# Moving one load to GpSimd's DMA queue and rebuilding the last transpose of the first chunk's output

## The chip, the cores and the metric

The kernel runs on one core of a Trainium2 chip. The metric is device microseconds of one execution, taken as the median of several. The engines of the core are named as in the profile: PE is TensorE (PEld its weight loads), DVE is VectorE, ACT is ScalarE, POOL is GpSimd, SP is SyncE. A "q" behind an engine's name (SPq, POOLq) is its sequencer, which issues DMAs.

## The reference, cut to what matters

An mLSTM cell over 4 batches, 8 heads, 768 time steps and head size 40, whose output feeds a two-layer network with a sigmoid-approximated GELU:

```
for t in range(S):                                    # S = 768, per batch and head
    m_new  = max(f[t] + m, i[t])
    f_stab = exp(f[t] + m - m_new); i_stab = exp(i[t] - m_new); m = m_new
    C = f_stab * C + i_stab * outer(v[t], k[t])       # 40 x 40
    n = f_stab * n + i_stab * k[t]
    y[t] = sigmoid(o[t]) * (C @ q[t]) / max(|n . q[t]|, 1)
x = y.transpose(0, 2, 1, 3).reshape(3072, 320)        # 8 heads x 40 = 320 features
h = x @ w_in                                          # 320 -> 2048
out = (h * sigmoid(1.702 * h)) @ w_out                # 2048 -> 320
```

All of it is in float32.

## The kernel before, in words

Time is cut into six chunks `w` of 128 steps. A chunk holds 4 batches of 128 steps, so 512 tokens, and 32 pairs of batch and head. Attention of a chunk is computed in matrix form (scores, weights, values and a carried state), and its output `y` (steps x 320 features, per batch) is turned into `xT` (features x tokens) for the network. While PE does the network of chunk `w`, the other engines prepare the attention of chunk `w + 1`. The order on every engine is written out by hand (`manual_schedule`): instructions stand on an engine in the order in which the program emits them.

**The first chunk's turn.** For `w = 0`, `outputs` writes `y` (L478), and `seam` transposes it on PE with the identity (L531): features 0, 2, 4, ... of the first 256, then 1, 3, 5, ..., then the last 64 features. The third transpose has 128 columns, because `outputs` also writes a copy of features 256 to 319 behind them (L482, on POOL, for the last batch on DVE). So the last 64 features come out twice, on partitions 0 to 63 and 64 to 127, as a later product wants them. All three transposes write one PSUM tile `p_x` of the pool `ps_a` (two buffers). ACT copies them to `xT` (L537). For the last batch DVE copies the first 128 columns (L534) and ACT the other 256 (L535). Then `up(0, 0)` starts the network: `full` (L620) runs over the halves `n` of the tokens, and half 1 of the very first weight block needs the last batch. Each such f32 product is two MATMUL rows in the profile. `rest` (L629) uses the last 64 features.

**The weights.** `w_in` and `w_out` come from DRAM with a wider layout and are rebuilt in 20 pieces by `convert`: two ACT operations (L243, L247) and four DVE operations (L256, L257, L259, L265) for a piece. Pieces 0 to 9 are `w_in`, 10 to 19 `w_out`. `fetch` issues their DMAs on SP.

**The loads.** SP issues nearly all of them, in the order of the program. Behind the first chunk's attention SP issues `load_gates(1)` (L92), `load(1, "k")` (L120), `load_squares(1, "q")` (L108), the first three `w_out` pieces (L167), and at `j == 1` of the network's loop `load(1, "v")` (L120), then further pieces, and at `j == 4` `spread(1)` (L403). Each DMA of an engine's queues takes the next of eight completion counts, and first waits until the DMA that held this count before it has landed; SP and ACT share one set of eight, POOL's queue has its own eight.

**POOL in this stretch.** At `j == 1` POOL runs `wait_for` (L586, it waits for a piece of `w_in`) and `scale(0, 1)` (L582, it reads `v_st`). At `j == 3` POOL's queue issues the DMAs of `gates(1)` (L304, L307, L330, L331) and of `columns_in(1)` (L350, L352), which lead to `columns_turn(1)` on DVE (L356).

**The queries of the second chunk.** `load_squares(1, "q")` fills the tile `q_sq` with four DMAs of 32 partitions x 16 x 160 numbers, 320 KB each. They are used by `block_transposes` on DVE (L394) at `j` 4 and 5, and twice more behind the loop.

Of the kernel before, what the change touches and what calls it, by code (L numbers as in the profile page):

```python
# [8 lines left out]
FP = mybir.dt.float32  # L9
# [8 lines left out]
L = 128  # L18
# [8 lines left out]
def kernel(  # L27
# [12 lines left out]
    nc = tc.nc  # L40
    B, H, S, D = q.shape
    BH = B * H
    DM = H * D
# [23 lines left out]
    ps_m = ctx.enter_context(tc.tile_pool(name="ps_m", bufs=4, space=PSUM))  # L67
    ctx.enter_context(tc.manual_schedule())

    V, A, G, T = nc.vector, nc.scalar, nc.gpsimd, nc.tensor  # L70
# [24 lines left out]
    def k_of(w):  # L95
        return (k_0, k_1)[w] if w < 2 else k_st[:, 0:BH * D].rearrange("s (h d) -> s h d", d=D)
# [2 lines left out]

        return k_of(w)[t, h, :] if w < 2 else k_st[t, h * D:h * D + DP]  # L100

    def load_squares(w, what):
        for dst, src in [((k_sq, k), (q_sq, q))["kq".index(c)] for c in what]:
            x = src[:, :, w * L:(w + 1) * L, :].rearrange("b (p two) (r c) d -> two r (b p) (c d)", two=2, c=4)
            for i in range(2):
                for n in range(2):
                    r, at = slice(i * 64 + n * 32, i * 64 + n * 32 + 32), (1 - n) * 32
                    nc.sync.dma_start(out=dst[r, at:at + BH // 2 * 4 * D].rearrange("r (j x) -> r j x", x=4 * D), in_=x[i])  # L108

    def load(w, what, bs=slice(0, B)):  # L110
        hs = slice(bs.start * H, bs.stop * H)
        for c in what:
            if c == "o" and w not in eo:
                eo[w] = ld.tile([L, BH, D], FP, tag="eo", bufs=1, name="eo")
            dst, src = {"k": (k_of(w), k), "q": (q_st, q), "v": (v_st, v), "o": (eo.get(w), o_gate)}[c]
            if w and c in "kv":
                for i, t, r in ((0, slice(0, L), slice(0, L)), (1, slice(0, HL), slice(HL, L)),
                                (1, slice(HL, L), slice(0, HL))):
                    x = src[:, :, w * L + t.start:w * L + t.stop, :].rearrange("b (p two) s d -> two s (b p) d", two=2)
                    nc.sync.dma_start(out=dst[r, i::2, 0:D], in_=x[i])  # L120
                continue
            nc.sync.dma_start(out=dst[:, hs, 0:D],
                              in_=src[bs, :, w * L:(w + 1) * L, :].rearrange("b h s d -> s (b h) d"))
# [74 lines left out]
    ident = const.tile([128, 128], FP, name="ident")  # L198
# [28 lines left out]
    kT, qT, ys, xT, gs, o_ps, sums, vw, x_row = {}, {}, {}, {}, {}, {}, {}, {}, {}  # L227
# [109 lines left out]
    def banks(name):  # L337
        return ps_a.tile([128, 2, 512], FP, tag="a", name=name)
# [125 lines left out]
    def outputs(w, hs, u):  # L464

        n = hs.stop - hs.start
        c, b = divmod(hs.start // H, 2)
        den = work.tile([L, n, 1], FP, tag="den", name="den")
        V.tensor_scalar(out=den, in0=u[:, :, D:D1], scalar1=-1.0, scalar2=1.0, op0=OP.mult, op1=OP.max)
        V.tensor_tensor(out=den, in0=u[:, :, D:D1], in1=den, op=OP.max)  # L470
        V.reciprocal(out=den, in_=den)
        z = eo[w][:, hs, :]
        V.scalar_tensor_tensor(out=z, in0=z, scalar=1.0, in1=u[:, :, 0:D], op0=OP.add, op1=OP.mult)
        if b == 0:
            ys[w, c] = work.tile([L, 2, DM + 64], FP, tag="y", name="y")
        for x in range(n // H):
            y, h = ys[w, c][:, b + x], slice(hs.start + x * H, hs.start + x * H + H)
            V.scalar_tensor_tensor(out=y[:, 0:DM].rearrange("p (h d) -> p h d", d=D), in0=eo[w][:, h, :], scalar=0.5,  # L478
                                   in1=den[:, x * H:(x + 1) * H].to_broadcast([L, H, D]), op0=OP.mult, op1=OP.mult)
        if w == 0:  # L480
            y = ys[w, c][:, b:b + n // H]
            (V if hs.stop == BH else G).tensor_copy(out=y[:, :, DM:DM + 64], in_=y[:, :, DM - 64:DM])  # L482

    def values(w, c):
        if w == 0:
# [35 lines left out]
    def x_of(w):  # L521
        if w not in xT:
            xT[w] = work.tile([128, 3, B, L], FP, tag="xT", bufs=1, name="xT")
        return xT[w]

    def seam(w, c, b):
        px = banks("p_x")[:, 0, 0:3 * L]
        y = ys[w, c][:, b, :]
        for x in range(3):
            y_x = y[:, 256:384] if x == 2 else y[:, x:256:2]  # L530
            T.transpose(px[:, x * L:(x + 1) * L], y_x, ident)  # L531
        to, px = x_of(w)[:, :, 2 * c + b, :], px.rearrange("r (x t) -> r x t", t=L)
        if 2 * c + b == B - 1:
            V.tensor_copy(out=to[:, 0], in_=px[:, 0])  # L534
            A.copy(out=to[:, 1:3], in_=px[:, 1:3])  # L535
        else:
            A.copy(out=to, in_=px)  # L537

    def x_square(c, n):

# [35 lines left out]
    def scale(w, c, part=0, parts=1):  # L576
        n = PH // parts
        hs = slice(c * PH + part * n, c * PH + (part + 1) * n)
        if part == 0:
            vw[w, c] = work.tile([L, PH, D1], FP, tag="u", name="vw")  # L580
        e = cols[w][:, 2 * BH + hs.start:2 * BH + hs.stop].unsqueeze(2).to_broadcast([L, n, D1])
        G.tensor_tensor(out=vw[w, c][:, part * n:(part + 1) * n], in0=v_st[:, hs, :], in1=e, op=OP.mult)  # L582
# [282 lines left out]
            convert_add(0)  # L865
    load_gates(1)
    load(1, "k")
    load_squares(1, "q")
    open_first(2)
    values(0, 2)  # L870
    open_first(3)
# [26 lines left out]
    for w in range(NW):  # L898
        more = w + 1 < NW
        if w == 0:  # L900
            for j in range(NF // 2):
                if j % 2 == 0:
                    ahead, behind = converted[j // 2]
                    run([(convert, p) for p in ahead] + [(fetch, p) for p in fetched.get(j // 2, ())])
                    up(w, j, lambda: run([(columns_turn, 1) if p is None else (convert, p) for p in behind]))
                if j == 6:
                    load(1, "o")
                if j == 1:
                    wait_for(w_in_sb[:, 1, 512:1024])
                    scale(0, 1)  # L910
                    load(1, "v")
                if j < B and j % 2:
                    carry(0, j // 2)
                if j == 3:
                    masks()
                    gates(1)
                    columns_in(1)
                if j == 4:
                    spread(1)
                if j >= B:  # L920
                    transposes(1, j - B)
                if j in (4, 5):
                    block_transposes(1, 2 * j - 7)
        else:
            token_sums(w)
            if more:
                gates(w + 1)
                load(w + 1, "o")
            for j in range(NF // 2):
                up_fast(w, j)  # L930
                if w == 1 and j < 4:
                    weight_sums(j)
                if more and j == 2:
                    load(w + 1, "vk")
                    columns_in(w + 1)
                    spread(w + 1)
                if more and j:
                    for n in ((), (0, 2), (4,), (6, 1), (3,), (5, 7), ())[j - 1]:
                        block_transposes(w + 1, n)
                if more and j == 7:  # L940
                    columns_turn(w + 1)
                if 2 <= j < 6:
                    hidden_difference(w, j - 2)
                if j >= 6:
                    hidden_sums(w, (j - 6,), G)
            gelu_fast(w, NF // 2 - 1)
            hidden_sums(w, (2, 3), V)
        side = attention(w + 1) if more else {}
        if w == 0:
            block_transposes(1, 5)  # L950
            block_transposes(1, 7)

            blocks = [(lambda b=b, n=n: down(w, b, n)) for n0 in (0, 2) for b in range(B) for n in (n0, n0 + 1)]
        else:
            blocks = down_fast(w, 0) + down_fast(w, 1)
        for i, block in enumerate(blocks):
            if w == 0 and i in (0, 4, 5):
                convert((17, 18, 19)[max(i - 3, 0)])
            if w + 2 < NW and i == (6 if w == 0 else 0):
                load_gates(w + 2)  # L960
            if w + 2 < NW and i == 13:
                load_squares(w + 2, "kq" if w else "k")
            if w == 0 and i == 15:
                load_squares(w + 2, "q")
            block()
            run(side.get(i, []))
            if w == 0 and i in (11, 13):
                input_sums(slice(0, 4) if i == 11 else slice(4, 8))
# [30 lines left out]
```

## Time and profile before

| what | us |
|---|---|
| median of three runs (468.34 to 468.99) | 468.94 |
| the profiled execution | 467.52 |
| its span, first to last instruction | 465.8 |
| PE busy in the span | 459.9 |
| DVE busy | 340.9 |
| ACT busy | 189.3 |
| POOL busy | 163.9 |
| mean granted TensorE clock | 1.000 |

The profile is one execution of the program; its own time is 1.72 us more than its span. Durations and instants below are of that execution, in us from the span's start. The span also comes in 40 slices of 11.6 us, in which a digit is the busy share of an engine in tenths. A row of the timeline gives the start, the length, the engine and line, the operation with its shape, how many instructions were merged, and in brackets how long the engine was idle before and what released it. The chain of waits is followed back from the last instruction, at each step to what released it.

### The profile page before, as it was taken

The page shows a single profiled execution, that of the slowest core. Times are in us where ns is not written, and L with a number is a line of the kernel's source. Part 1 is how long each engine was busy: PE and PEld are TensorE (multiplying, and loading weights), DVE is VectorE, ACT ScalarE, POOL GpSimd, SP SyncE. Part 2 cuts the span into 40 slices and gives each one's busy share as a digit, 9 for nine tenths or more (in the row PEclk, how much of TensorE's full clock was granted, in tenths as well). Part 3 has the DMA queues.
Part 4 walks back from the last instruction along what each step waited for, and adds up shares of the span by engine and source line. Part 5 has one row for each costly group of instructions (what it writes and reads, how often), then busy time and mean ns, then how long its engine had stood idle before and what let it go on. Part 6 is the DMA issues. An engine that isn't in the chain of part 4 may idle for free.

```text
span 465.8 us, 12359 instructions
## 1 busy us (share of the span) xinstructions
PE 459.9 (99%) x5063; PEld 387.9 (83%) x5063; DVE 340.9 (73%) x699; ACT 189.3 (41%) x431; POOL 163.9 (35%) x153
## 2 busy tenths in 40 slices
PE   8999999999999999999999999999999999999996
PEld 6867887776769999678999678999878999877996
DVE  5788999799779777688875688876768867535622
ACT  4676769200546500554700554900444810354100
POOL 5101417100898600365700266700248510157100
PEclk9999999999999999999999999999999999999999
DMA  8999998049993036997024998024999305000000
GB/s 166 210 308 159 206 301 180 3 94 185 156 154 97 14 76 141 188 134 139 3 65 127 194 136 161 6 56 103 198 136 107 90 18 139 28 1 0 1 29 30
DMA packets 135561, 52.87 MB, mean 113 GB/s; under 512 B 101984, under 2 KB 131632, under 8 KB 135504
## 3 DMA queue, kind: packets, MB, share of 16 engines
q1 hardware_dynamic: 127136, 50.27, 54.9%
q10 hardware_dynamic: 8048, 1.66, 1.8%
q8 instruction: 40, 0.66, 0.7%
q0 software_dynamic: 320, 0.15, 0.2%
q14 instruction: 17, 0.14, 0.1%
HBM read 44.52 MB, written 7.54 MB: 112 GB/s over the span
## 4 chain that ended last, share of the span: by engine, by line
PE 94%; SPq 1%; DVE 1%; POOL 1%; DMA 1%; ACT 0%; issue 0%; DVEq 0%
PE p_out L812 33%; PE p_h L703 25%; PE p_h L711 8%; PE p_out L758 8%; PE p_h L620 6%; PE p_c L596 3%; PE p_o L503 2%; PE p_s L459 2%; PE p_i L511 2%; PE p_h L629 2%; PE p_t L386 1%; PE p_s L448 1%; SPq L120 1%; DMA k_sq<-in_k_dram 1%; PE p_o L493 0%; PE p_w L415 0%
## 5 line engine op out<-in xcount | busy, mean ns | idle before, releaser
L749 POOL TENSOR_TENSOR g<-g,parts 128x512 f32<-128x512 f32 x30 | 38.3, 1278 | 190.2 <-DVE parts L741 182.8
L737 ACT COPY parts<-p_h 128x256 f32<-128x256 f32 x40 | 14.9, 373 | 150.3 <-PE p_h L703 147.0
L812 PE MATMUL p_out<-w_out_sb,g 128*128 128x160 f32 x480 | 69.6, 301 | 0.1
L812 PEld LDWEIGHTS p_out<-w_out_sb,g 128*128 128x128 f32 x480 | 66.5, 190 | 1.2 <-ACT g L684 0.4
L703 PE MATMUL p_h<-xT,w_in_sb 128*128 128x256 f32 x240 | 67.0, 388 | 0.0
L684 ACT ACTIVATE g<-g 128x512 f32<-128x512 f32 x80 | 50.1, 631 | 40.0 <-DVE g L744 24.2
L703 PEld LDWEIGHTS p_h<-xT,w_in_sb 128*128 128x128 f32 x240 | 43.8, 190 | 18.5 <-issue 7.5
L817 DVE TENSOR_TENSOR o_sb<-o_sb,p_out 128x160 f32<-128x160 f32 x70 | 21.4, 317 | 41.1 <-PE p_out L812 40.5
L812 PE MATMUL p_out<-t_sb,s 128*128 128x160 f32 x320 | 47.2, 300 | 0.0
L740 DVE TENSOR_TENSOR t_x<-p_h,parts 128x256 f32<-128x256 f32 x40 | 16.7, 418 | 39.3 <-PE p_h L711 33.2
L812 PEld LDWEIGHTS p_out<-t_sb,s 128*128 128x128 f32 x320 | 44.4, 190 | 0.2
L703 PE MATMUL p_h<-t_x,s_in 128*128 128x256 f32 x160 | 41.1, 379 | 0.0
L711 PE MATMUL p_h<-xT,w_in_x 64*128 64x512 f32 (+1 forms) x192 | 39.8, 540 | 0.0
L435 ACT ACTIVATE wt<-wt,cols 128x64 f32<-128x64 f32 x160 | 38.8, 333 | 0.1
L758 PE MATMUL p_out<-w_out_sb,g 128*128 128x320 f32 x128 | 35.7, 436 | 0.0
L703 PEld LDWEIGHTS p_h<-t_x,s_in 128*128 128x128 f32 x160 | 30.4, 190 | 4.2
L758 PEld LDWEIGHTS p_out<-w_out_sb,g 128*128 128x128 f32 x128 | 23.9, 190 | 9.5
L741 DVE TENSOR_TENSOR parts<-p_h,t_x 128x512 f32<-128x512 f32 x40 | 27.7, 692 | 3.6
L748 ACT COPY g<-p_h 128x512 f32<-128x512 f32 x30 | 17.4, 580 | 30.7 <-PE p_h L711 25.3
L620 PE MATMUL p_h<-xT,w_in_sb 128*128 128x256 f32 x128 | 29.8, 385 | 0.0
L711 PEld LDWEIGHTS p_h<-xT,w_in_x 64*128 64x128 f32 x192 | 16.9, 186 | 14.7 <-issue 13.7
L744 DVE TENSOR_TENSOR g<-p_h,parts 128x512 f32<-128x512 f32 x40 | 27.7, 691 | 1.4
(197 smaller groups left out, 841.1 us busy)
## 6 DMA issues: line engine op xcount, KB each, us to landing
q_sq<-in_q_dram SPq DMA_DIRECT2D x20, 320.0 KB, 10.2
wt<-m_row SPq DMA_DIRECT2D x20, 256.0 KB, 5.5
k_sq<-in_k_dram SPq DMA_DIRECT2D x16, 320.0 KB, 6.0
out_dram<-o_sb SPq DMA_DIRECT2D x24, 160.0 KB, 1.9
eo<-in_o_gate_dram SPq DMA_DIRECT2D x5, 640.0 KB, 8.1
bits<-in_moe_w_in_dram SPq DMA_DIRECT2D x6, 512.0 KB, 10.5
q_sq<-x_row SPq DMA_DIRECT2D x10, 256.0 KB, 2.8
v_st<-in_v_dram SPq DMA_DIRECT2D x14, 160.0 KB, 5.1
```

Of the source, the lines that this page charges most:

```text
L435: A.activation(out=x[:, h, :], in_=x[:, h, :], func=AF.Exp, scale=-1.0, bias=cols[w][:, c * PH + h:c * PH + h + 1])
L620: T.matmul(ph[j][i][:, t], w_in_sb[:, c, f * 128:(f + 1) * 128], x[:, c, t], start=(first and c == 0 and n == 0), stop=(not first and c == ...
L684: A.activation(out=gs[w, j][:, i, :], in_=gs[w, j][:, i, :], func=AF.Gelu_apprx_sigmoid)
L703: T.matmul(out, a, x[n], start=start, stop=stop)
L711: T.matmul(row[:, t], w_in_x[r, j, :], rest_x[r, 2, t], start=(not late and h == 0), stop=(late and h == n - 1))
L741: V.tensor_tensor(out=y[:, half_w:3 * half_w].rearrange("p (a t) -> p a t", a=2), in0=flat[:, half_w:3 * half_w].rearrange("p (a t) -> p a ...
L744: V.tensor_tensor(out=g[:, 1, :], in0=row1, in1=y[:, half_w:3 * half_w], op=OP.add)
L748: A.copy(out=g[:, 0, :], in_=row0)
L749: G.tensor_tensor(out=g0, in0=g0, in1=u, op=OP.add)
L758: T.matmul(po, gs[w, f // 2][:, f % 2, b * L:(b + 1) * L], w_out_sb[:, f, :], start=(f == 0), stop=(f == NF - 1))
L812: T.matmul(po, a(f), b[:, f, :], start=(f == 0), stop=(f == NH - 1))
L817: V.tensor_tensor(out=dst, in0=x, in1=po, op=OP.add)
```

## The change

Three edits. The load of the second chunk's queries leaves SP's queue and is issued by POOL's queue, behind `scale(0, 1)` at `j == 1`. DVE's copy of the last 64 features in `outputs` goes for the last batch of the first chunk. And `seam` has a path of its own for that batch: the first transpose writes a PSUM tile of the pool `ps_m` (four buffers), the second writes `p_x`, the third takes only 64 columns; ACT then copies the second with one operation, and the third with two, once to partitions 0 to 63 and once to 64 to 127.

```diff
-    def load_squares(w, what):
+    def load_squares(w, what, queue=nc.sync):
...
-                    nc.sync.dma_start(out=dst[r, at:at + BH // 2 * 4 * D].rearrange("r (j x) -> r j x", x=4 * D), in_=x[i])
+                    queue.dma_start(out=dst[r, at:at + BH // 2 * 4 * D].rearrange("r (j x) -> r j x", x=4 * D), in_=x[i])
...
-        if w == 0:
+        if w == 0 and hs.stop < BH:
             y = ys[w, c][:, b:b + n // H]
-            (V if hs.stop == BH else G).tensor_copy(out=y[:, :, DM:DM + 64], in_=y[:, :, DM - 64:DM])
+            G.tensor_copy(out=y[:, :, DM:DM + 64], in_=y[:, :, DM - 64:DM])
...
     def seam(w, c, b):
+        y, to = ys[w, c][:, b, :], x_of(w)[:, :, 2 * c + b, :]
+        if 2 * c + b == B - 1:
+            first = ps_m.tile([128, L], FP, tag="m", name="p_x")
+            T.transpose(first, y[:, 0:256:2], ident)
+            px = banks("p_x")[:, 0, 0:2 * L]
+            T.transpose(px[:, 0:L], y[:, 1:256:2], ident)
+            T.transpose(px[0:64, L:2 * L], y[:, 256:DM], ident)
+            V.tensor_copy(out=to[:, 0], in_=first)
+            A.copy(out=to[:, 1], in_=px[:, 0:L])
+            for r in (0, 64):
+                A.copy(out=to[r:r + 64, 2], in_=px[0:64, L:2 * L])
+            return
         px = banks("p_x")[:, 0, 0:3 * L]
-        y = ys[w, c][:, b, :]
         for x in range(3):
             y_x = y[:, 256:384] if x == 2 else y[:, x:256:2]
             T.transpose(px[:, x * L:(x + 1) * L], y_x, ident)
-        to, px = x_of(w)[:, :, 2 * c + b, :], px.rearrange("r (x t) -> r x t", t=L)
-        if 2 * c + b == B - 1:
-            V.tensor_copy(out=to[:, 0], in_=px[:, 0])
-            A.copy(out=to[:, 1:3], in_=px[:, 1:3])
-        else:
-            A.copy(out=to, in_=px)
+        A.copy(out=to, in_=px.rearrange("r (x t) -> r x t", t=L))
...
     load_gates(1)
     load(1, "k")
-    load_squares(1, "q")
     open_first(2)
...
                     wait_for(w_in_sb[:, 1, 512:1024])
                     scale(0, 1)
+                    load_squares(1, "q", G)
                     load(1, "v")
```

## The prediction, made before the changed kernel was run

> **What bounds the kernel now.** I read the page first: shares of the span, then slices.
>
> ```profile
> PE 459.9 (99%) x5063; PEld 387.9 (83%) x5063; DVE 340.9 (73%) x699; ACT 189.3 (41%) x431; POOL 163.9 (35%) x153
> PE   8999999999999999999999999999999999999996
> DMA  8999998049993036997024998024999305000000
> ```
>
> PE works through every slice but the first and last; the DMA engines are full in the first six. So time can be won where PE stands still, or lost by making PE wait. The second view, the busy time by stages, says where PE stands still (busy us and instruction counts of PE, PEld, DVE, ACT, POOL; then clock, DMA share, GB/s):
>
> ```profile
> 0.00:27.16 27.16, 24.92 (x314) 19.33 (x314) 17.95 (x53) 15.11 (x31) 8.80 (x27) 1.00 0.95 215
> 27.16:110.50 83.34, 83.34 (x895) 63.40 (x896) 73.81 (x140) 45.33 (x98) 18.12 (x20) 1.00 0.74 168
> ```
>
> From 27.16 to 110.50 PE has no gap. Both moved loads and all their users lie in there. Ahead of 27.16 PE lacks 2.24 us, most of it at the start. What is left is the turn. Third view, the chain of waits around it, in order of time:
>
> ```profile
> 25.46 0.50 DVE y L478
> 25.96 0.14 issue
> 26.10 0.59 PE p_x L531 x3
> 26.68 0.43 PE p_h L620 x2
> 27.12 0.04 issue
> 27.16 4.99 PE p_h L620 x22
> ```
>
> And the timeline of the same instants:
>
> ```profile
> 25.98 0.19 DVE L482 COPY y<-y 128x64 f32<-128x64 f32 x1
> 26.72 0.29 DVE L534 COPY xT<-p_x 128x128 f32<-128x128 f32 x1 [0.54 <-PE p_x L531]
> 27.05 0.37 ACT L535 COPY xT<-p_x 128x256 f32<-128x256 f32 x1 [0.62 <-DVE xT L534]
> 27.13 0.30 PEld L620 LDWEIGHTS p_h<-xT,w_in_sb 128*128 128x128 f32 x2 [0.41 <-issue]
> ```
>
> DVE's copy L534 starts when all three transposes are through (26.69), ACT's only when DVE has left the tile (27.01). PE has done half 0 of the first block (two rows from 26.52) and starts half 1 at 27.16, 0.15 behind L534's end. Rows of L620 follow each other every 0.227 (4.99 / 22), so without a wait half 1 would start at 26.52 + 0.454 = 26.97.
>
> **The change part by part.**
>
> *DVE's copy L482 (0.19).* It ended at 26.17; DVE then sat idle until 26.72 for the transposes. Worth nothing on the path: the transposes hide it. Without that cover it would be 0.19.
>
> *The third transpose.* 64 columns for 128. The three rows of L531 took 0.59 together, some 0.13 to 0.2 of pitch each; half a weight load less is between 0 and 0.1; I take 0.05. So half 0 starts at 26.47.
>
> *The separate tile.* The instruction order of the changed kernel shows DVE's copy waiting for the first transpose alone. That one starts at 26.10 and takes 0.27 to 0.39 by the rows of L531 (median 0.283), so the copy runs from 26.42 (0.03 for the release, as now) to 26.71, and half 1 may start at 26.71 + 0.15 = 26.86. PE itself is there at 26.47 + 0.454 = 26.92. PE no longer waits, and half 1 starts 0.24 earlier. Bounds: with nothing from the smaller transpose it is 26.97, 0.19 earlier; with 0.1 from it 26.87, 0.29 earlier. I take 0.24.
>
> *ACT's three copies for one.* 128x384 took 0.48 and 128x256 0.373, so 128 columns cost about 0.27, with a pitch of 0.17 to 0.27 (the two L537 in a row: 0.86 for 2 x 0.48). They start behind the third transpose, at about 26.67 rather than 27.05, and end at 27.28 to 27.5, against 27.42. The first user of the second 128 features is the 17th row of L620, at 26.47 + 16 x 0.227 = 30.1; of the last 64, L629 near 31.9. Cover 2.6 us or more. ACT's next, L247, feeds DVE's L265 (now 28.67): no later than now. If that cover went, it would cost at most 0.2.
>
> *What is late next.* DVE's conversions start 0.30 earlier (L256 follows L534), so `w_in_x` is ready at about 31.4, for 31.72 now, and L629 wants it at about 31.85. Pieces 3 and 4 (ready 36.42) stand before 36.98 and move likewise. The new tile shifts the round of four `ps_m` buffers by one: the fourth product tile now waits for DVE's copy (26.71) and is first written by row 13, near 29.2. Nothing in PE's next 83 us binds, so the 0.24 travels to the end.
>
> *SP without the four q issues (2.74 us, 38.37 to 41.11).* The `w_out` pieces, the v load, the next pieces and the spread move forward by up to that. ACT waited for such DMAs 1.19 us (until 50.15) and 3.82 us (until 61.98), and those waits shrink; but PE did not wait in that stretch, so this is worth 0. v's tile is free once POOL's L582 ends at 38.04. Late k would cost: PE transposes it from 56.2, it lands by about 44 now, and even all 1.28 MB of q ahead of it, at the stage's 168 GB/s, is 8 us.
>
> *POOL with the four issues.* They stand behind `scale(0, 1)`, so from about 38.05. Nothing on POOL is queued behind them until 50.12:
>
> ```profile
> 36.76 1.28 POOL L582 TENSOR_TENSOR vw<-v_st,cols 128x656 f32<-128x656 f32 x1
> 50.12 0.68 POOL L304 DMA_DIRECT2D m_row<-m_run  x1 [12.08 <-DVE m_run L296]
> 52.45 0.70 POOL L330 DMA_DIRECT2D st_row<-f_run  x1
> 56.38 2.42 POOL L350 DMA_DIRECT2D raw<-st_row  x4 [2.72 <-DMA st_row<-f_run]
> 57.10 0.43 DVE L257 TENSOR_SCALAR w_out_sb<-w_out_sb 128x512 uint32<-128x512 uint32 x1
> 61.35 2.06 DVE L394 STREAM_TRANSPOSE qT<-q_sq 128x512 f32<-128x512 f32 x2
> ```
>
> POOL's issues in this trace take 0.52 to 1.15 each, the nearest in pieces being L330 with 384 runs of 128 bytes (0.70); a q load has 512 runs of 640 bytes. Four are 2.1 to 4.6 us, I take 3: done at 41, 9 us before L304. Landing: L330 took 3.6 us, the q loads on SP 5.8 to 8.3 here and 10.2 in the median of all. I take 10: the last lands near 51. Bounds 42 and 55. Who needs them: DVE's L394 at 61.35, and, by the turns on eight counts, L331 at 53.15 waits for the first q load and the four L350 at 56.38 for the others. Both behind the expected landing. If L350 were late, L356 on DVE (70.31) would be next; its data now land at about 65.
>
> *DVE beside POOL's issues.* L257 at 36.80 took 1.53, not 0.43: it stood behind POOL's L582. POOL's DMA issues do not show that: L257 at 57.10, in the middle of L350, took 0.43, and the issues stayed at 0.55 to 0.80. The Trainium skill, "SBUF — State Buffer", section "Who interferes with whom", speaks against this edit: GpSimd writes the descriptors of its DMAs through a port that such VectorE operations lock, and the loser waits. By it q could lag by a few operations of 0.43, estimated at 4 x 0.43 = 1.7 us, still inside the cover, so its sum would be the same. From the rows alone: even four DVE operations held up for a whole 0.70 (2.8 us) meet 1.22 us of DVE idle at 42.2 and piece 9, ready 54.38 for 57.27 on PE.
>
> Sum: 0 + 0.24 + 0 + 0 = 0.24 us. The profiled execution would take 467.52 - 0.24 = 467.28. It lay 1.42 below the median of the runs shown, so on that scale 468.94 - 0.24 = 468.70.
>
> **The rivals.** A measurement of this kernel can tell about 0.2% from no change, 0.94 us.
>
> *Slower: POOL's queue delivers q late.* The place is DVE's L394. It stalls from 61.35, and behind it stand pieces 13 and 14 of `w_out`. Piece 14 is ready at 68.03 (its L265) and PE, whose first 32 rows of L758 take 8.62 from 67.34, wants it with the 13th, at 67.34 + 12 x 0.269 = 70.57. So it decides from a landing at 61.35 + 2.5 = 63.9, 26 us after the issue, and each us beyond is one of the kernel: at 30 us of transfer about 4 us, 473. For it: DMA digits of 9 in slices 1 to 5 (11.6 to 69.9), a queue that moved only 0.15 MB so far, and the same counts that chain L331 and L350 to q. Against: 3.6 to 6.2 us to landing on that queue in the same stretch, and 20 us of cover. 15%.
>
> *Faster beyond 0.94: SP's relief reaches PE.* Only if the 5.0 us of ACT waits fed a gap of PE; between 27.16 and 110.50 it has none, in the next stage 0.15 us. By the rows it is 0.24 + 0.15 at most, 468.55. What could carry it over is what the rows don't explain: the profiled execution lay 1.42 us below the median. A median moved by 0.7 to 1 gives about 467.8. 14%.
>
> *It does not do what it says: L534 still ends last.* If the copy is no earlier, half 1 stays at 27.16 or PE is set by another release: 468.9. 11%, inside 0.2%.
>
> **How the numbers follow.** The forecast (0.1 to 0.4 us won, 468.5 to 468.85, and the scatter of 0.65 between runs around it) has 60%. With the third rival, within 0.2% has 71%. Faster 14%, slower 15%. To hold 8 in 10 the range takes all within 0.2% and the near part of both other cases: 467.8 to 470.2, the upper end being q 1.5 us behind the deciding point.
>
> **What would show it.** Right: DVE's 128x128 copy starts near 26.4, ACT's first of three starts near 26.7, no longer behind DVE's, L620 rows follow every 0.227 from the first; POOLq has four q issues from 38 to 41; the `w_out` issues start near 38.4; POOL's `m_row` issue stays near 50; the stage from 27 to 110 shows no PE gap. Wrong: a stall of DVE ahead of the query transposes near 61, `raw` issues later than 57, or a PE gap between 56 and 90.

## The result, and the profile after

| | median, us | range | runs |
|---|---|---|---|
| before | 469.00 | 467.33 to 473.87 | 20 |
| after | 469.78 | 467.39 to 475.33 | 20 |

The ratio is 1.0015, with a 95% interval from 0.9994 to 1.0037: no difference that this measurement can tell. The profiled execution of the changed kernel took 469.14 us, its span 467.4.

The page, read as before: shares of the span, and the slices.

```profile
PE 460.4 (99%) x5063; PEld 387.4 (83%) x5063; DVE 341.7 (73%) x698; ACT 189.6 (41%) x433; POOL 165.2 (35%) x157
PE   8999999999999999999999999999999999999997
DMA  8999999028995034988124999114999405000000
```

At this scale PE looks the same; of the DMA digits, the seventh is 9 where it was 8, and some later ones move too. The busy time by stages shows more (columns as before):

```profile
0.00:27.16 27.16, 25.07 (x318) 19.52 (x319) 18.75 (x54) 16.26 (x34) 8.90 (x27) 1.00 0.93 192
27.16:110.50 83.34, 81.70 (x884) 61.23 (x883) 71.61 (x133) 44.29 (x97) 19.67 (x24) 1.00 0.79 171
```

PE had no gap in the second stretch; now it lacks 1.64 us (83.34 less 81.70). The timeline of the turn shows that the turn is not to blame:

```profile
24.69 0.49 DVE L478 SCALAR_TENSOR_TENSOR y<-eo,den 128x320 f32<-128x320 f32 x1
...
25.24 0.38 PE L530 MATMUL p_x<-ident,y 128*128 128x128 f32 x1 [0.47 <-DVE y L478]
...
25.66 0.29 DVE L534 COPY xT<-p_x 128x128 f32<-128x128 f32 x1 [0.48 <-PE p_x L530]
...
25.89 0.27 ACT L535 COPY xT<-p_x 128x128 f32<-128x128 f32 x1 [0.22 <-PE p_x L533]
26.05 0.53 ACT L537 COPY xT<-p_x 64x128 f32<-64x128 f32 x2
```

DVE's copy waits for the first transpose (L530) alone, and ACT's copies no longer for DVE. The chain of waits has the 24 rows of the first block in one piece, where before it had two rows, a stop and 22:

```profile
25.85 5.23 PE p_h L626 x24
```

From the end of `y` (25.19) to the end of the 24 rows (31.08) are 5.89 us. Before, they were 6.19 (25.96 to 32.15). The turn won 0.30.

So where does PE stand? The waits of PE from 56 to 90 (us in total, times, longest), and behind them the chain of the same stretch, cut to its DMA and the steps that follow it:

```profile
PE p_out L764 <- ACT g L641: 0.7, 1, 0.7
PE p_c L602 <- POOL vw L588: 0.5, 1, 0.5
PE p_out L764 <- DVE w_out_sb L265: 0.3, 1, 0.3
```

```profile
60.67 5.14 DMA bits<-in_moe_w_out_dram
...
74.06 0.58 ACT t_sb L247
...
75.95 0.27 ACT cols L367
...
77.61 1.29 POOL vw L588
...
78.94 1.14 PE p_c L602 x64
```

Read it from the bottom. PE's carry (L602) waits for POOL's `vw`, which waits for the columns that ACT makes (L367). ACT works in order, and the columns stand behind its conversions of the `w_out` pieces 13 to 17; the first of these waits for its DMA until 65.8 (before: until 61.98). The same lateness holds ACT's gelu (L641) back, which PE wants at 67. Before, the carry (there L596) followed the product without a gap, with `vw` ready in time. This is the chain before:

```profile
67.34 8.62 PE p_out L758 x32
75.96 2.01 PE p_c L596 x128
```

SP's issues after, and two of its rows before, show when the pieces go out:

```profile
40.60 11.81 SPq L167 DMA_DIRECT2D s_in<-in_moe_w_out_dram  x7
53.31 6.13 SPq L120 DMA_DIRECT2D v_st<-in_v_dram  x3
59.49 6.33 SPq L167 DMA_DIRECT2D bits<-in_moe_w_out_dram  x10
65.87 0.43 SPq L167 DMA_DIRECT2D t_sb<-in_moe_w_out_dram  x1
```

```profile
48.96 5.44 SPq L120 DMA_DIRECT2D v_st<-in_v_dram  x3
54.46 7.43 SPq L167 DMA_DIRECT2D bits<-in_moe_w_out_dram  x10
```

Relieved of the four query issues, SP should have been early. Instead the seven `w_out` issues took 11.81 us (before: 6.66), v followed at 53.31 (before: 48.96), the pieces 13 to 17 (`bits`, `t_sb`) at 59.49 and 65.87 (before: 54.46 and 61.93).

Busy time hides part of this: short waits lie inside the merged rows (the 16 rows of L635 took 2.54 us, where L629 before took 2.00; the carry 2.40 for 2.08). A cleaner yardstick, used below, is the **stretch**: from the start of the last `y` (L478) to PE's first product behind the carry (L758, in kernels with the new turn L764). Before, it ran from 25.46 to 77.89, so 52.43 us; after, from 24.69 to 80.01, so 55.32.

### The profile page after: what moved, and what is told of

Its sections match the earlier page's. It is cut to its first block, busy times and chain, and to the rows that moved or that the text cites. A ratio compares the mean times of both kernels' runs of the same rounds, so it can differ in the third digit from the quotient of the medians.

```text
span 467.4 us, 12367 instructions
## 1 busy us (share of the span) xinstructions
PE 460.4 (99%) x5063; PEld 387.4 (83%) x5063; DVE 341.7 (73%) x698; ACT 189.6 (41%) x433; POOL 165.2 (35%) x157
## 3 DMA queue, kind: packets, MB, share of 16 engines
q1 hardware_dynamic: 125024, 48.96, 54.3%
## 4 chain that ended last, share of the span: by engine, by line
PE 92%; ACT 2%; POOL 1%; DMA 1%; issue 1%; SPq 1%; DVE 1%; POOLq 0%; ACTq 0%; DVEq 0%
PE p_out L818 33%; PE p_h L709 27%; PE p_h L717 8%; PE p_out L764 6%; PE p_h L626 5%; PE p_c L602 2%; PE p_o L503 2%; PE p_s L459 2%; PE p_i L511 2%; PE p_h L635 1%; DMA bits<-in_moe_w_out_dram 1%; PE p_t L386 1%; PE p_s L448 1%; SPq L120 1%; ACT w_out_sb L243 0%
## 5 line engine op out<-in xcount | busy, mean ns | idle before, releaser
L764 PE MATMUL p_out<-w_out_sb,g 128*128 128x320 f32 x128 | 36.1, 437 | 1.0 <-ACT g L641 0.7
L764 PEld LDWEIGHTS p_out<-w_out_sb,g 128*128 128x128 f32 x128 | 23.9, 190 | 11.1 <-ACT g L641 0.9
L626 PE MATMUL p_h<-xT,w_in_sb 128*128 128x256 f32 x128 | 29.7, 385 | 0.0
```

Source lines behind the costliest of these rows:

```text
L626: T.matmul(ph[j][i][:, t], w_in_sb[:, c, f * 128:(f + 1) * 128], x[:, c, t], start=(first and c == 0 and n == 0), stop=(not first and c == ...
L764: T.matmul(po, gs[w, f // 2][:, f % 2, b * L:(b + 1) * L], w_out_sb[:, f, :], start=(f == 0), stop=(f == NF - 1))
```

## The experiments

**First round: each half, and both kernels again.** Theory A: the transfers of the first chunk are a second bound, and queries issued on POOL's queue, beside the others, make the pieces late. Theory B: both kernels scatter in this stretch, and the profile of before was a lucky one. Theory C: POOL's issues hold DVE up.

`before_again` and `after_again` have no edit. `seam_only` is the kernel before with the new turn and without the copy; `q_only` is the kernel before with this alone:

```diff
-    load_squares(1, "q")
...
                     scale(0, 1)
+                    load_squares(1, "q", G)
                     load(1, "v")
```

> The kernel before, unchanged, for the scatter between executions. Theory A (crowding): in the changed kernel POOL's query loads share the DMA engines with the second chunk's keys and the first w_out pieces that SP issues; the keys land late, SP's queue, which waits for the DMA eight back, falls behind, the w_out pieces come some 4 us late and PE stands still for 1 to 3 us between 60 and 80 us. By A this run looks like the first profile of before: the 160 KB key loads land within 4 to 9 us, the first v load is issued near 49, PE has no gap above 0.3 us from 30 to 110. Rival B (scatter): the late DMAs of the changed kernel's profile were one slow execution; by B this run may show them as well, a first v load at 51 or later and PE gaps of 1 us or more. Time ratio to before 1.000, interval within 0.003 of it.

> The changed kernel, unchanged, a second look. A: again the 160 KB key loads take 12 us or more to land, the first v load is issued at 52 or later, ACT's first w_out conversion waits for its DMA, PE stands still for 1 to 3 us in sum between 56 and 80. B: the DMAs may be on time, and then PE has no gap there and the span is 0.2 to 0.4 us under that of before. Time ratio 1.000 to 1.004 by A, 0.999 to 1.000 by B.

> The turn of the changed kernel, the query load back on SP at its old place. Both theories: no wait between the first two rows and the later rows of the first product after the turn, 0.2 to 0.3 us won against before from the end of y to row 3; PE without a gap above 0.3 us to 110; the first v load issued near 49. Time ratio 0.998 to 1.000.

> The query load on POOL's queue, the turn as before. A: keys and w_out pieces late as in the changed kernel, the first v load at 52 or later, PE gaps of 1 to 3 us between 56 and 80, ratio 1.002 to 1.006. B: nothing but scatter, ratio 1.000, no PE gap. A third theory C, that POOL's descriptor writing holds up DVE, would show DVE's two-port operations between 37 and 41 much longer than 0.43 and DVE, not a DMA, as the releaser of PE's waits.

| | median, us | ratio to before, 95% | start of `y` | stretch | mean clock |
|---|---|---|---|---|---|
| before_again | 468.73 | 0.9981 [0.9958, 1.0003] | 24.37 | 53.62 | 1.000 |
| after_again | 469.87 | 1.0001 [0.9975, 1.0028] | 25.25 | 55.60 | 0.993 |
| seam_only | 469.05 | 0.9985 [0.9963, 1.0008] | 25.06 | 53.87 | 1.000 |
| q_only | 469.67 | 1.0010 [0.9980, 1.0040] | 25.44 | 57.72 | 0.992 |

All ratios include 1, so the times alone tell nothing. As for the traces, B is half right: before_again, the same code, has a stretch 1.2 us longer than the first profile of before, and `y` itself starts anywhere from 24.4 to 25.5, which is more than the turn can win. A has the two longest stretches, both with the queries on POOL's queue. Their first `w_out` issues did come early, at 38.44 and 38.91 (before_again 41.65), but the loads took 9.8 to 13.6 us to land (before_again 5.9 to 9.4), and the second v issue stood until the last v issue at 54.34 and 55.67 (before_again 54.17): SP's lead was gone. Yet this doesn't show A. These two executions were the second slowest and the slowest of the 12 of their kernel (471.99 and 473.40 us), and before_again's was the second fastest (467.57). Signs that A had named failed too: the keys of after_again landed after 6.9 to 10.1 us, not 12 or more; the first v load went out at 44.31 and 46.16, not at 52 or later; and seam_only, for which both theories wanted a v load near 49 and no PE gap above 0.3 us, issued it at 51.58 and had a gap of 0.7. C has no row behind it: no wait of PE above 0.4 us ends on DVE.

**Second round: lighten the load, or move its victim.** `no_q` drops the added line from the changed kernel, so that the queries are not loaded at all. The three `early_cols` kernels (on the kernel before, on seam_only, on the kernel after) put DVE's transposition of the columns ahead of its work on pieces 14 to 16, and piece 17 behind the columns in ACT's order:

```diff
-    converted = {0: ((3, 4), (5,)), 1: ((6,), (7, 8)), 2: ((9, 10), (11, 12)), 3: ((13,), (14, 15, None, 16))}
+    converted = {0: ((3, 4), (5,)), 1: ((6,), (7, 8)), 2: ((9, 10), (11, 12)), 3: ((13,), (None, 14, 15, 16))}
...
-            if w == 0 and i in (0, 4, 5):
+            if w == 0 and i in (1, 4, 5):
```

> The changed kernel without the second chunk's query load: that chunk is computed with what the first chunk's queries left in the tile. Theory A, as the first runs sharpened it: between 37 and 80 us the DMA engines set the pace. SP is relieved of the query issues, but the next loads' waits for the DMA eight back, and the engines' share that POOL's loads take, hand the 2.7 us back at the v load; w_out pieces 13 to 17 then land 2 to 4 us later, ACT takes them in order and computes the second chunk's columns behind piece 17, so POOL's value scaling and PE's carried state near 77 wait. With 1.28 MB less to move, pieces 13 to 17 are 4 us earlier, PE has no gap above 0.3 us from 30 to 110, and the span is 2 us or more under that of the changed kernel, near 465; ratio to before 0.995 to 0.999. Rival B (scatter of the DMAs, whatever is loaded): PE gaps near 77 as in the other runs, ratio 1.000.

> The kernel before, with the second chunk's columns taken out from behind the late w_out pieces: DVE's transpose of the columns ahead of pieces 14 and 15, and ACT's piece 17 one block later, behind the columns. A: the columns no longer wait for pieces 14 to 17, POOL's value scaling starts 2 to 4 us earlier, no PE gap at the carried state, the time of before's undisturbed executions or a little less: ratio 0.997 to 1.000. B: no difference, 1.000.

> The new turn, the query load on SP, and the early columns. A: nothing behind the turn gives its gain back; no gap of PE at the carried state, so 0.2 to 0.3 us under early_cols_before between equal starts, ratio to before 0.996 to 0.999. B: as seam_only.

> The changed kernel, whole, with the early columns. A: the late pieces no longer hold the carried state; the PE gap near 77 falls from 1 to 3 us to under 0.5, TensorE's granted clock stays at 1.00 there, and the ratio to before is 0.997 to 1.000, where the changed kernel had 1.0015 and 1.0001. B: as the changed kernel, 1.000 to 1.002.

| | median, us | ratio to before, 95% | start of `y` | stretch |
|---|---|---|---|---|
| no_q | 466.25 | 0.9947 [0.9929, 0.9966] | 25.29 | 52.14 |
| early_cols_before | 468.44 | 0.9988 [0.9964, 1.0011] | 24.91 | 52.45 |
| early_cols_seam | 469.18 | 0.9986 [0.9959, 1.0012] | 24.45 | 54.24 |
| early_cols_after | 468.46 | 0.9993 [0.9973, 1.0013] | 25.27 | 53.11 |

`no_q` is the first that is clearly faster: without the 1.28 MB of queries PE has no gap, and the runs lie between 466.0 and 466.8. So the load of the queries is what holds the stretch back; whether its place matters, this can't tell. With the early columns the wait at the carry is 0.6 us in early_cols_after (0.5 and 2.1 in the two profiles of the changed kernel; under 0.5 was expected) and none in early_cols_seam (0.7 in seam_only), but there PE waited 0.9 us for ACT's gelu and 0.5 us for DVE's `w_out_sb` instead: all of ACT's queue is late, not the columns alone. No gain in time is shown.

**Third round: the turn by itself, and queue against place.** `no_queries_new_turn` repeats no_q. `no_queries_old_turn` takes `load_squares(1, "q")` out of the kernel before, so that the two differ by the turn alone, with the transfers out of the way. `queries_on_sync_later` issues the queries where the change does, but on SP. `queries_gpsimd_after_keys` lets POOL wait for the keys first:

```diff
-                    load_squares(1, "q", G)
+                    wait_for(k_1[:, BH - 1, :]); wait_for(k_1[:, BH - 2, :]); load_squares(1, "q", G)
```

> Leaves out the second chunk's query load (the second chunk is computed with the queries that lie there), with the new turn. A repeat of the earlier run, to be set beside the next kernel. If the transfers of the first chunk are the second bound (theory A): no PE gap between 27.16 and 110.50 (PE busy 83.34 of 83.34), median 466.0 to 466.6, ratio 0.993 to 0.997. If the earlier run was luck of the draw (theory B): a gap of 0.5 us or more, and 467.5 to 469.

> The kernel before with the second chunk's query load left out (its place in the sums is taken by the queries that lie there), and the old turn. With the transfers eased, nothing but the turn differs from the kernel run beside it. If the turn's gain reaches the end where no transfer binds (theory A): 0.2 to 0.4 us slower than that kernel, about 466.5, from y to the end of 24 rows of L620 and L626 about 6.2 us for 5.9. If the gain is swallowed before or behind the turn whatever the transfers do (the rival): the two medians agree within 0.15 us.

> The changed kernel, with the four query issues at the changed place in the order but on SyncE's queue: behind the first w_out pieces, ahead of v. Two readings of what the GpSimd queue did are told apart. If two queues side by side hand the engines' share to the 640-byte runs and away from the 160-byte ones (A1): k's halves land 5 to 8 us after issue, 8.2 to 8.6 MB are moved from 37 to 74 us, the PE gap is 0.3 to 1 us, the clock stays at 1.00, ratio 0.996 to 0.999. If only the sum of bytes counts, wherever they are issued (A2): the same gap as the changed kernel's repeats, 1.5 to 3 us, ratio 0.999 to 1.002.

> The changed kernel, but GpSimd waits until the second chunk's keys have landed before it issues the four query loads. A1 (sharing between the queues costs the 160-byte runs): the keys land 5 to 8 us after issue, the query issues start at 43 to 45, the first w_out pieces go out at 38 and land in 6 to 9 us, 8.0 to 8.4 MB are moved from 37 to 74 us, the PE gap is under 1 us, ratio 0.996 to 1.000. A2 (the sum of bytes): a gap of 1.5 us or more, 7.6 to 7.9 MB, ratio 0.999 to 1.002. Either way the queries, landing near 55 to 57, push the raw issues to 57 to 60 and do not hold DVE's L394.

| | median, us | ratio to before, 95% | start of `y` | stretch |
|---|---|---|---|---|
| no_queries_new_turn | 466.44 | 0.9933 [0.9911, 0.9956] | 25.07 | 52.14 |
| no_queries_old_turn | 466.68 | 0.9946 [0.9927, 0.9964] | 24.95 | 52.44 |
| queries_on_sync_later | 468.78 | 0.9996 [0.9971, 1.0021] | 25.28 | 56.51 |
| queries_gpsimd_after_keys | 470.10 | 1.0012 [0.9986, 1.0037] | 25.24 | 55.21 |

The first two are the cleanest pair of the study. Without the queries in the way their runs spread by only about 1 us (9 runs from 465.94 to 466.84, 12 from 466.18 to 467.33), and the new turn is 0.24 us faster in the median, 0.30 in the mean, with a standard error of 0.14 worked out from these runs, so that it is only just clear of zero (95%: 0.03 to 0.57). The timelines of the two agree. New turn, then old:

```profile
25.07 0.49 DVE L478 SCALAR_TENSOR_TENSOR y<-eo,den 128x320 f32<-128x320 f32 x1
...
77.21 6.73 PE L764 MATMUL p_out<-w_out_sb,g 128*128 128x320 f32 x24
```

```profile
24.95 0.49 DVE L478 SCALAR_TENSOR_TENSOR y<-eo,den 128x320 f32<-128x320 f32 x1
...
77.39 6.73 PE L758 MATMUL p_out<-w_out_sb,g 128*128 128x320 f32 x24
```

52.14 against 52.44 us. The two floors recur to 0.01 us: 52.14 in both executions without queries that have the new turn; 52.43 to 52.45 in no_queries_old_turn, early_cols_before and the first profile of before. What an execution lies above its floor is put down here to the transfers; in after_again and q_only it includes 1.3 and 1.6 us for a carry at half the clock (see the last section).

The other pair was to tell the queue from the place. A1, that POOL's queue takes the share of the engines from SP's, expected SP's own queue to restore 8.2 to 8.6 MB from 37 to 74 us and a gap of at most 1 us. It moved 7.5 MB, and PE lacked 3.56 us. So this execution needed no second queue for a long stretch. It shows no more than that: it was the second slowest of 12 (471.46), their median, 468.78, is under that of before, and the interval of the ratio overlaps what A1 expected as well as what A2 did. A2, that only the sum of bytes counts, has the gap here, and in queries_gpsimd_after_keys too (7.7 MB, 2.26 us lacking). The two profiled executions of before move the same bytes and sit 0 and 1.2 us above their floor, but an ordinary run of before takes 2.5 us more than one without the queries (469.22 against 466.68), so this doesn't speak against A2. Nor do the four kernels with a long stretch share a place: queries_on_sync_later and queries_gpsimd_after_keys issue the queries behind the first `w_out` pieces, the changed kernel and q_only beside or ahead of them, from 36.93 to 37.97 (before: 38.37). SP's issues in queries_on_sync_later show how a late stretch comes about:

```profile
38.50 3.85 SPq L167 DMA_DIRECT2D s_in<-in_moe_w_out_dram  x7
43.98 2.17 SPq L108 DMA_DIRECT2D q_sq<-in_q_dram  x4
46.69 10.38 SPq L120 DMA_DIRECT2D v_st<-in_v_dram  x3
57.12 8.31 SPq L167 DMA_DIRECT2D bits<-in_moe_w_out_dram  x10
```

The `w_out` pieces 10 to 12 were early and landed after only 5.4 to 7.5 us, but the three v issues took 10.38 us (before: 5.44), the second alone 6.81 us, from 49.54 to 56.35, while the last two query loads ahead of it landed at 55.2 and 56.8; and the pieces 13 to 17 stood behind them. So SP is held while the loads ahead are under way. It isn't the completion count: the load eight back, the 64 KB of `w_out` issued at 40.98, had landed at 47.0, before this issue began. Whether room in the queue holds it, no run here tests. In queries_gpsimd_after_keys the keys landed after 5.9 to 9.7 us and w_out after 5.4 to 6.0, as A1 wanted, and yet the second and third v load needed 14.2 and 13.9 us, the first `bits` issue then took 8.30, and the next came at 58.22.

The executions with the columns at their usual place, sorted by where the queries are issued (the first two rows load none). The time is that of the profiled execution, with the median of its kernel's runs:

| queries | kernel | piece 17 first issued | landed | columns (L367) | above the floor, us | time (median) |
|---|---|---|---|---|---|---|
| not loaded (new turn) | no_queries_new_turn | 56.60 | 65.6 | 70.19 | 0 | 466.62 (466.44) |
| not loaded (old turn) | no_queries_old_turn | 53.90 | 61.5 | 70.38 | 0 | 466.79 (466.68) |
| SP, behind the keys | before | 61.93 | 69.2 | 72.26 | 0 | 467.52 (469.00) |
| | before_again | 63.59 | 71.3 | 73.93 | 1.2 | 467.57 (468.73) |
| | seam_only | 64.66 | 71.9 | 74.88 | 1.7 | 468.54 (469.05) |
| SP, behind w_out 10 to 12 | queries_on_sync_later | 65.47 | 74.4 | 77.56 | 4.4 | 471.46 (468.78) |
| POOL, behind `scale` | after | 65.87 | 72.5 | 75.95 | 3.2 | 469.14 (469.78) |
| | after_again | 64.00 | 72.5 | 75.80 | 3.5 | 471.99 (469.87) |
| | q_only | 64.78 | 74.9 | 77.83 | 5.3 | 473.40 (469.67) |
| POOL, behind the keys | queries_gpsimd_after_keys | 65.53 | 72.9 | 76.14 | 3.1 | 469.58 (470.10) |

The way from the transfers to PE stands in all eight executions that load the queries: the columns come 2.6 to 3.4 us behind the landing of piece 17, and by and large the later they are, the longer is the stretch. (The floor is 52.43 with the old turn and 52.14 with the new.) What a place costs can't be read from the table. The five executions of moved queries lie from 3.1 to 5.3 above the floor and the three with the old place from 0 to 1.7, but each is one draw: the three fast ones lie 0.5 to 1.5 us under the median of their kernel, three of the five slow ones 2.1 to 3.7 above it. The medians hardly differ, 468.73 to 469.86 with the queries at their old place (before, as run beside each round, included) and 468.78 to 470.10 elsewhere, and every interval includes 1. In time, the whole comparison of after against before is 0.8 us in the medians, with an interval that includes none. The three early_cols executions lie at 0, 2.1 and 1.0, the last with moved queries.

So the load of the queries costs an ordinary run some us wherever it is issued (in the medians of the last round 2.5 in before, 2.3 in queries_on_sync_later, 3.7 in queries_gpsimd_after_keys); that moving it costs anything further is not shown. No kernel that loads everything was shown to beat both.

## Why the prediction was right, and which step failed

The forecast, no difference that can be told, held, and 469.78 lies in the range. In part that was luck: the 0.1 to 0.4 us that it expected to win (468.5 to 468.85) did not show, and what swallows them, a second bound, was not in the prediction. Whether the moved load adds a cost of its own stays open.

- **The separate tile, the third transpose, the copy: right.** L534 starts 0.42 us behind the start of its one transpose, predicted 0.32; ACT's copies begin 0.70 us behind the end of `y`, predicted 0.71, and end at 26.58, far ahead of their first user; L620's rows (here L626) without a stop. Predicted 0.24 (0.19 to 0.29); 0.30 in the traces of before and after, 0.30 between the floors, 0.24 in the medians of the pair without queries. The working slipped by at most 0.06.
- **"Nothing in PE's next 83 us binds, so the 0.24 travels to the end": the step that failed.** It travels where the transfers are light (the pair without queries). With the queries loaded, ACT's waits for `w_out` pieces decide when PE gets its carry: PE lacks 1.64 us in the profile after, and the query load hangs 2.5 us on an ordinary run of before. By the chain, an earlier PE then only waits longer; the times are too scattered to show this by itself.
- **SP's relief, pieces "move forward by up to that": wrong.** The first `w_out` issues came 2 to 3 us earlier in two executions of three (38.44 and 38.91, against 41.21 and 41.65), but their loads took longer to land, SP stood at the second v load while they were under way, and the pieces behind it went out no earlier: piece 17 at 64.00 to 65.87, in before and before_again at 61.93 and 63.59. ACT's wait for piece 13, which was to shrink, ended at 65.8 in the profile after, for 61.98. The prediction had followed what is chained to the queries on POOL's queue, L331 and L350, but not what stands behind v on SP's.
- **The cover was read in one execution, and that one was at its floor.** The prediction noticed that the profiled execution lay 1.42 us below the median and that no row explained it. This was the clue: an ordinary execution of before has a PE wait that this profile doesn't show (even before_again, a fast one, lies 1.2 us above the floor). In the last round the median of before was 469.22, and 466.68 without its queries, so some 2.5 us of an ordinary run hang on that load.
- **POOL's side: right.** Four issues in 2.77 us (3 taken), from 36.93; 5.2 to 12.4 us to landing (10 taken); DVE's L394 was never held. One detail was misread: three of the four L350 take counts that queries held, the fourth that of `m_row`. This is the timeline of POOL in the kernel after:

```profile
36.93 2.77 POOL L108 DMA_DIRECT2D q_sq<-in_q_dram  x4
...
57.17 2.18 POOL L350 DMA_DIRECT2D raw<-st_row  x4 [4.71 <-DMA st_row<-f_run]
```

- **Late keys: thinner than read.** The prediction had them land by about 44, and with all of q ahead of them 8 us later, against a use at 56.2. In after_again it was 44.2, but 53.2 in the profile after, 2 us ahead of the use at 55.34.
- **DVE beside POOL's issues: small.** L256 and L257 at 38.74 and 39.34 took 0.57 and 0.61 instead of 0.41 and 0.43, the same in after_again and q_only. The rule of the Trainium skill that the prediction weighed ("SBUF — State Buffer", "Who interferes with whom") has the loser of the shared port wait for the whole instruction; here the two operations were 0.34 us longer together, beside issues of 0.65 to 0.84 each, and off the path. The lag of the queries that the prediction estimated from it, 1.7 us, is not to be seen in any run by itself.
- **The rivals.** Slower for queries that reach DVE late: not so. Whether the change is slower by a mechanism near it, with another victim, not the reader of the queries but the loads behind them, is not shown. "SP's relief reaches PE" has no support. "L534 no earlier" is refuted. Of the signs set out as wrong, the PE gap between 56 and 90 and `raw` later than 57 (57.17) both came in the profile after.

## What to carry to other kernels

A stage in which the DMA engines are full can have two bounds, and an engine's 100% in one profile says only that the other bound did not win in that execution; compare its time with the median, and if it lies below, profile again before calling a wait covered. The same holds for sorting kernels by one profile each: a fast draw of one and a slow draw of another look like a difference. When a load is moved past others, follow the loads that it will land beside and those that stand behind them in their queue, to their last user, and not only the load that moves: here, in the profile after, the queries were on time and the weights were late. Measure a small gain with the noisy neighbour taken out: without the queries 0.24 us could be seen, in runs that otherwise spread over 4.

## What was not expected of the hardware

In two executions PE's gap cost more than its length. The busy time by stages of after_again:

```profile
72.00:78.00 6.00, 3.92 (x45) 2.56 (x44) 5.76 (x10) 5.93 (x16) 1.80 (x2) 1.00 1.07 283
78.00:84.00 6.00, 6.00 (x118) 4.87 (x111) 5.66 (x8) 6.00 (x27) 5.77 (x5) 0.51 0.67 100
```

Behind a gap of 2.1 us (72 to 78) the granted clock is 0.51 for the next six (the last columns are clock, DMA share, GB/s). The 128 rows of the carry took 3.38 us instead of 2.08, the 24 rows of L764 behind them 8.74 instead of 6.73: some 3 us more. q_only, with a gap of 3.0 us, shows the same (0.50 from 80 to 84). But queries_on_sync_later had a gap of 2.57 us and kept its clock at 1.00, so the length of the gap alone doesn't decide. The Trainium skill, "TensorE: Matmul & The Clock Gate", section "Part 1: The HAM clock gate (the "warmup" mystery)", has the clock fall to half after an idle window of about 3.4 us, and the window run free of the kernel; that the same gap can fall differently into it would fit both outcomes, but gaps shorter than the window already did it here, and no run here shows where the windows lay. It makes the long runs plausible, no more: of the runs of before beside the last round, three of the four above 470.8 have a mean clock of 0.995 or 0.996, and one has 1.000; of the 20 runs after, the four above 472 have 0.992 or 0.993.
